# The same steps of an attention and feed-forward kernel, issued in a new order that holds 53 matmuls on zeros fewer

## The chip, the cores and the metric

The kernel runs on one core of one Trainium2 chip. Each core has five engines that work side by side: TensorE (PE, matmuls; its weight loads are shown apart as PEld), VectorE (DVE), ScalarE (ACT), GpSimd (POOL), and SyncE (SP), which here issues the transfers (DMAs). Each engine takes its instructions in the order in which the program issued them and waits where an operand isn't ready yet; engines meet only at such waits. The metric is device time in microseconds (us), median of several runs; less is better.

## The reference

Attention over a local window and a few global keys, with the result as the input of a feed-forward net:

```
q, k, v: (B=4, H=8, S=768, D=64) f32;  n_global = 8, n_local = 96
scores = q @ k^T / sqrt(D)
keep   = (key < n_global) | (0 <= query - key < n_local)
dist   = n_local where a key is global and not local, else |query - key|
scores = where(keep, scores - 2^-(h+1) * dist, -1e9)
a      = exp(scores - max(scores));  a = a / (sum(a) + 1e-9)
x      = (a @ v), heads side by side: (3072 tokens, 512)
h      = x @ w_in                                   # w_in (512, 2048)
g      = where(h >= 1, h, where(h <= -1, 0, (h + 1)^2 / 4))
out    = g @ w_out                                  # w_out (2048, 512)
```

`moe_w_in` and `moe_w_out` arrive as 64-bit floats, which the kernel takes apart as pairs of 32-bit words.

## The kernel before

**Halves.** A 32-bit product is made of three 16-bit ones: each operand is split into a high and a low f16 half, and high x high, high x low and low x high are summed in PSUM. The engines besides TensorE spend much of their work on splitting.

**Units and chunks.** The tokens lie in 24 units of 128 (one block of 128 queries of one batch, all eight heads); each unit has two halves of four heads. Two units make a chunk of 256 tokens for the feed-forward part, so there are 12 chunks.

**Steps.** Function `fast_path` doesn't issue instructions as it goes. It collects a list `plan` of steps, each a time, a function and its arguments, sorts the list by time (2808 steps), and then issues the steps in the order that the constant `PLACE` (L103) gives, a list of indices into the sorted plan:

```
1033    for n in PLACE or range(len(plan)):
1034        t, _, f, args = plan[n]
1037        f(*args)
```

So `PLACE` alone sets the order of each engine's queue. An index that it leaves out isn't issued. Which step runs on which engine:

- Weights: 32 pieces (0 to 15 of `w_in`, 16 to 31 of `w_out`). `w_load` (SP, L466) fetches a piece into one of three raw buffers; `w_bits` makes 32-bit floats of it in three DVE steps (L480, L484, L487) of 128x512; `w_hi` (ACT, L500) rounds to the high half, `w_scale` (ACT, L507) scales, `w_lo` (POOL, L514) subtracts to the low half. `check_load` (SP) and `check_reduce` (DVE, L546) read all weights once more to look at their range.
- Units 0 to 3 go a short way in f32: `first_scores` (8 matmuls, L567), `masked` (DVE, L578, bias, mask and maximum of one head), `expo` (ACT, L590), `norm` (two small DVE steps, L602 and L604), `first_turn` (four transposes on TensorE, L616), `first_pt` (ACT), `first_av` (8 matmuls, L634), `scale_x` (DVE, L642), `first_xt` (two transposes), `first_x` (ACT and DVE). `slope`, `positions`, `limits`, `distances` and `clip` build the bias.
- Units 4 to 23: `fetch` (SP), `conv_hi` (ACT), `conv_lo` (POOL L712 and L713, for v DVE L707), `keep_glob` and `set_glob` (DVE L740, L742) for the global keys; then `scores` (24 matmuls, L757), `masked`, `expo`, `norm`, `split_p` (ACT L773, then DVE L775), `turn_p` (SP, a transposing DMA, L782), `attend` (24 matmuls, L800), `scale_x`, `split_x` (ACT L814, DVE L816), `turn_x` (SP, a transposing DMA, L824).
- Feed-forward part: `ffn1(c,g)` (24 matmuls of 256 columns, L885, eight g in each chunk c) reads the transposed x of both units and two weight pieces; `gelu(c,g,s)` in five steps (ACT L898, DVE L903, DVE L908, ACT L912, POOL L916); `ffn2(c,t,f)` (three matmuls of 512 columns, L928; t is the unit of the chunk, f runs to 15) sums into PSUM; `finish` scales and stores.
- `filler` (L448) is one matmul of 512 columns on a tile of zeros into the tile `spare` (L443), whose result nobody reads; `warm` issues the same. The plan holds 150 `filler` steps, of which `PLACE` issues 101; eight `warm` calls of one matmul each come on top.

In this text `attend(5,0)` means that step for unit 5, half 0, and so on. The second `spare` tile serves as a buffer for every other `w_in` piece in `w_bits`, and in the rows on the tile `spare` these DVE steps stand under DVE.

**The first stage.** In the order before, TensorE has `positions`, `limits`, six `filler`, `first_scores(0,0)`, one `filler`, `first_scores(0,1)`, `first_turn(0,0)`, `first_turn(0,1)`, `first_av(0,0)`, `first_scores(1,0)`, one `filler`, `first_xt(0,0)`, seven `filler`, `first_av(0,1)`, and so on, with runs of up to 11 `filler` between the steps until about 75 us. `ffn1` begins at 32.04, `ffn2` of the first chunk at 75, and `ffn1` of the second at 80. The first `scores` of unit 4 stands at 100.3, the first `attend` at 126.45, and the last weight piece's `w_lo` at 120.7.

Of the kernel before, what the change touches and what calls it, by code (L numbers as in the profile page):

```python
# [103 lines left out]
    3, 0, 1, 2, 5, 7, 8, 71, 9, 4, 72, 11, 73, 74, 37, 6, 231, 300, 75, 10, 12, 13, 14, 19, 15, 16, 17, 18, 20,  # L104
    23, 76, 22, 21, 24, 27, 30, 25, 28, 32, 35, 34, 33, 29, 39, 45, 38, 41, 40, 48, 55, 49, 26, 36, 57, 31, 42,
    46, 54, 43, 47, 44, 52, 50, 53, 51, 334, 56, 223, 58, 77, 60, 78, 62, 63, 79, 59, 80, 81, 69, 64, 70, 82,
    61, 67, 359, 66, 65, 221, 83, 68, 227, 224, 241, 244, 225, 222, 240, 242, 84, 233, 226, 261, 234, 247, 236,
    238, 235, 228, 232, 289, 85, 237, 86, 248, 87, 243, 229, 290, 88, 246, 89, 230, 90, 249, 91, 250, 262, 239,
    253, 256, 92, 259, 394, 254, 260, 257, 245, 93, 94, 255, 263, 251, 266, 264, 268, 265, 252, 275, 269, 258,
    299, 270, 267, 95, 96, 302, 273, 272, 274, 305, 309, 97, 311, 278, 98, 347, 277, 360, 308, 286, 363, 279,  # L110
    313, 368, 365, 99, 315, 271, 422, 280, 100, 317, 372, 101, 276, 102, 366, 103, 373, 104, 282, 105, 375, 106,
    281, 291, 378, 326, 284, 285, 327, 385, 388, 288, 296, 318, 283, 413, 322, 287, 450, 107, 418, 331, 292,
    301, 108, 109, 421, 335, 110, 295, 111, 293, 294, 341, 298, 112, 304, 113, 114, 342, 297, 314, 115, 116,
    117, 310, 118, 119, 120, 303, 320, 325, 344, 307, 312, 329, 306, 319, 420, 316, 427, 330, 424, 321, 430,
    350, 336, 323, 328, 324, 426, 332, 333, 337, 431, 346, 338, 454, 339, 485, 340, 345, 121, 510, 343, 349,
    122, 123, 124, 348, 352, 357, 379, 440, 457, 351, 362, 125, 126, 356, 382, 127, 353, 355, 128, 129, 354,
    364, 391, 361, 130, 358, 131, 462, 132, 376, 133, 370, 134, 135, 136, 367, 380, 383, 369, 371, 374, 389,
    395, 381, 377, 392, 441, 459, 384, 467, 399, 386, 396, 390, 409, 387, 464, 393, 397, 398, 400, 407, 468,
    402, 401, 404, 406, 137, 138, 403, 410, 537, 433, 405, 411, 538, 419, 408, 139, 539, 140, 438, 141, 465,
    142, 412, 425, 416, 443, 414, 471, 143, 417, 144, 415, 145, 429, 146, 428, 147, 148, 423, 149, 150, 437,  # L120
    151, 432, 152, 153, 434, 439, 444, 445, 435, 436, 447, 446, 442, 448, 449, 478, 549, 451, 452, 470, 453,
    455, 590, 593, 456, 591, 598, 458, 154, 155, 461, 460, 466, 156, 157, 463, 473, 472, 480, 474, 553, 610,
    158, 603, 159, 160, 475, 161, 162, 163, 614, 469, 484, 481, 557, 164, 476, 487, 165, 166, 167, 479, 560,
    483, 168, 482, 169, 477, 170, 489, 171, 488, 486, 492, 607, 563, 515, 490, 633, 566, 494, 493, 517, 568,
    572, 491, 574, 498, 499, 495, 496, 500, 502, 497, 617, 503, 501, 577, 628, 504, 637, 507, 644, 505, 521,
    506, 508, 512, 511, 524, 669, 509, 518, 513, 527, 514, 651, 522, 523, 520, 519, 670, 526, 516, 654, 525,
    534, 528, 540, 530, 541, 542, 529, 664, 533, 543, 547, 531, 532, 658, 551, 536, 546, 555, 701, 535, 713,
    558, 704, 552, 698, 544, 718, 705, 545, 570, 564, 550, 556, 548, 575, 721, 579, 742, 567, 554, 583, 586,
    559, 571, 671, 752, 562, 565, 561, 576, 573, 569, 763, 585, 578, 600, 710, 580, 605, 589, 753, 770, 609,
    581, 595, 584, 582, 588, 615, 754, 587, 619, 785, 599, 592, 601, 596, 594, 597, 606, 604, 602, 630, 618,  # L130
    608, 811, 634, 611, 622, 639, 613, 612, 616, 623, 640, 621, 641, 620, 643, 652, 629, 647, 650, 624, 631,
    657, 649, 627, 635, 625, 636, 655, 638, 661, 653, 672, 663, 626, 660, 675, 747, 666, 632, 662, 681, 751,
    642, 680, 739, 682, 648, 645, 684, 741, 659, 690, 646, 694, 744, 683, 656, 691, 686, 674, 665, 673, 695,
    668, 667, 749, 712, 677, 678, 717, 676, 781, 679, 860, 692, 792, 685, 732, 697, 688, 687, 689, 702, 693,
    699, 696, 700, 715, 706, 703, 723, 707, 729, 708, 714, 711, 789, 727, 709, 735, 724, 716, 736, 743, 745,
    719, 734, 748, 726, 720, 722, 730, 756, 725, 738, 728, 760, 731, 750, 740, 733, 762, 757, 767, 755, 764,
    737, 766, 769, 758, 772, 768, 746, 773, 774, 759, 771, 761, 776, 775, 777, 780, 787, 779, 783, 784, 782,
    778, 791, 820, 765, 786, 788, 796, 790, 793, 799, 821, 804, 945, 823, 794, 946, 835, 827, 798, 795, 847,
    816, 805, 797, 814, 800, 810, 806, 801, 809, 817, 802, 803, 857, 808, 807, 813, 812, 851, 840, 815, 818,
    824, 819, 822, 859, 886, 861, 889, 825, 828, 833, 882, 826, 865, 831, 829, 978, 838, 845, 830, 832, 980,  # L140
    842, 837, 836, 841, 839, 844, 843, 862, 834, 846, 848, 984, 850, 849, 986, 852, 854, 912, 853, 855, 856,
    858, 863, 992, 864, 867, 866, 911, 915, 869, 871, 868, 936, 870, 874, 872, 878, 875, 876, 997, 879, 873,
    914, 880, 877, 995, 883, 891, 885, 881, 892, 938, 888, 884, 940, 893, 897, 887, 898, 890, 894, 904, 895,
    896, 917, 922, 899, 919, 1013, 920, 900, 1014, 907, 901, 923, 1021, 902, 906, 909, 903, 905, 910, 916, 996,
    908, 1023, 1015, 913, 918, 921, 961, 963, 924, 925, 928, 926, 933, 927, 929, 931, 930, 934, 942, 932, 1044,
    937, 947, 935, 1050, 948, 944, 1053, 951, 939, 941, 943, 1066, 950, 949, 956, 1063, 952, 1070, 953, 954,
    1075, 957, 958, 955, 1076, 964, 960, 959, 967, 966, 1026, 968, 1082, 962, 1089, 969, 965, 971, 998, 972,
    999, 970, 974, 1001, 973, 1002, 976, 1005, 1000, 975, 1004, 1003, 982, 977, 1108, 1007, 985, 979, 1109,
    1049, 1051, 1008, 981, 983, 1117, 1006, 1012, 989, 1009, 987, 991, 1119, 1010, 1020, 1011, 1016, 988, 1125,
    990, 993, 994, 1017, 1024, 1018, 1142, 1025, 1019, 1027, 1022, 1032, 1028, 1031, 1037, 1029, 1057, 1036,  # L150
    1033, 1038, 1040, 1043, 1060, 1041, 1046, 1148, 1100, 1101, 1030, 1047, 1152, 1034, 1045, 1058, 1035, 1077,
    1039, 1156, 1042, 1173, 1159, 1174, 1048, 1061, 1069, 1054, 1052, 1055, 1056, 1064, 1059, 1176, 1067, 1062,
    1072, 1065, 1073, 1068, 1074, 1071, 1083, 1078, 1081, 1088, 1079, 1087, 1090, 1205, 1084, 1095, 1092, 1206,
    1093, 1097, 1098, 1147, 1149, 1080, 1096, 1106, 1085, 1086, 1099, 1116, 1091, 1122, 1103, 1094, 1214, 1102,
    1104, 1110, 1124, 1112, 1105, 1150, 1114, 1216, 1107, 1111, 1120, 1113, 1237, 1121, 1115, 1123, 1118, 1130,
    1126, 1129, 1135, 1127, 1243, 1134, 1131, 1136, 1138, 1141, 1246, 1175, 1139, 1144, 1250, 1128, 1145, 1253,
    1195, 1196, 1132, 1143, 1157, 1133, 1265, 1137, 1140, 1266, 1146, 1160, 1166, 1268, 1153, 1151, 1154, 1155,
    1162, 1158, 1164, 1161, 1168, 1163, 1171, 1165, 1172, 1167, 1169, 1177, 1180, 1170, 1179, 1178, 1184, 1297,
    1183, 1185, 1181, 1188, 1186, 1187, 1298, 1191, 1192, 1242, 1244, 1182, 1189, 1203, 1190, 1306, 1194, 1193,
    1213, 1198, 1199, 1201, 1197, 1200, 1208, 1219, 1209, 1202, 1210, 1308, 1204, 1211, 1212, 1215, 1221, 1329,  # L160
    1224, 1223, 1229, 1231, 1226, 1227, 1236, 1233, 1234, 1267, 1228, 1239, 1335, 1207, 1289, 1247, 1240, 1290,
    1338, 1248, 1251, 1342, 1345, 1222, 1217, 1249, 1260, 1359, 1232, 1238, 1218, 1360, 1235, 1252, 1241, 1362,
    1255, 1220, 1257, 1245, 1225, 1254, 1256, 1230, 1258, 1259, 1262, 1261, 1263, 1269, 1264, 1391, 1270, 1272,
    1392, 1273, 1274, 1279, 1277, 1278, 1281, 1282, 1284, 1286, 1271, 1287, 1334, 1336, 1275, 1285, 1295, 1276,
# [1059 lines left out]
```

## Time and profile before

| what | value |
|---|---|
| runs | 628.42, 631.13, 628.40 us |
| median | 628.42 us |
| span of the profiled execution | 629.1 us |
| instructions | 14881 |
| TensorE busy | 615.7 us (98%) |
| DVE, ACT, POOL busy | 448.0, 418.7, 239.5 us |
| DMA | 88.08 MB, mean 140 GB/s |

The span is the time from the first to the last record of one profiled execution, 0.7 us above the median of the runs, which were timed without it. The profile gives each engine's busy time, the clock that TensorE was granted (1.00 is its full level of 2.4 GHz), and for each group of instructions what ended the idle time before it. Busy time is an average over stages with different limits, so views of single stretches are read beside it.

### The profile page before, as it was taken

The page shows a single profiled execution, that of the slowest core. Times are in us where ns is not written, and L with a number is a line of the kernel's source. Part 1 is how long each engine was busy: PE and PEld are TensorE (multiplying, and loading weights), DVE is VectorE, ACT ScalarE, POOL GpSimd, SP SyncE. Part 2 cuts the span into 40 slices and gives each one's busy share as a digit, 9 for nine tenths or more (in the row PEclk, how much of TensorE's full clock was granted, in tenths as well). Part 3 has the DMA queues.
Part 4 walks back from the last instruction along what each step waited for, and adds up shares of the span by engine and source line. Part 5 has one row for each costly group of instructions (what it writes and reads, how often), then busy time and mean ns, then how long its engine had stood idle before and what let it go on. Part 6 is the DMA issues. An engine that isn't in the chain of part 4 may idle for free. (4 is left out here: it accounts for less than half of the span.)

```text
span 629.1 us, 14881 instructions
## 1 busy us (share of the span) xinstructions
PE 615.7 (98%) x5665; PEld 420.8 (67%) x5665; DVE 448.0 (71%) x1150; ACT 418.7 (67%) x1070; POOL 239.5 (38%) x226
## 2 busy tenths in 40 slices
PE   7999999899999999999999999999999999999996
PEld 4676666556876767767757667667667767767652
DVE  6889999987676656665777777777777686663440
ACT  4778898997777776676686776766866765632220
POOL 0336786650544424433443333425324421122210
PEclk9999999999999999999999999999999999999999
DMA  6847566597533553464395497586476455361121
GB/s 201 261 144 225 187 227 221 129 170 157 126 87 77 91 121 93 80 148 111 69 231 154 94 208 186 127 186 175 110 177 183 112 140 137 76 150 69 51 69 38
DMA packets 144227, 88.08 MB, mean 140 GB/s; under 512 B 108180, under 2 KB 124820, under 8 KB 144148
## 3 DMA queue, kind: packets, MB, share of 16 engines
q1 hardware_dynamic: 144000, 86.92, 55.4%
q8 instruction: 46, 0.75, 0.5%
q14 instruction: 33, 0.27, 0.1%
q10 hardware_dynamic: 148, 0.13, 0.1%
HBM read 54.53 MB, written 6.29 MB: 97 GB/s over the span
## 5 line engine op out<-in xcount | busy, mean ns | idle before, releaser
L885 PE MATMUL h<-xt,wih 128*128 128x256 f16 x1536 | 256.4, 273 | 1.0 <-DVE u L908 0.9
L916 POOL TENSOR_TENSOR gl<-u,gh 128x512 f16<-128x512 f32 x96 | 117.4, 1224 | 284.9 <-ACT gh L912 274.6
L885 PE MATMUL h<-xt,wil 128*128 128x256 f16 x768 | 209.4, 273 | 0.0
L885 PEld LDWEIGHTS <-wih 128*128 128x128 f16 x1536 | 147.4, 98 | 30.9 <-DVE u L908 1.6
L928 PE MATMUL o<-wol,gh 128*128 128x512 f16 x384 | 145.6, 379 | 1.3 <-POOL wol L514 1.2
L928 PE MATMUL o<-woh,gh 128*128 128x512 f16 x384 | 145.8, 380 | 0.0
L928 PE MATMUL o<-woh,gl 128*128 128x512 f16 x384 | 145.6, 379 | 0.0
L928 PEld LDWEIGHTS <-gh 128*128 128x128 f16 x768 | 71.8, 98 | 67.3
L903 DVE SCALAR_TENSOR_TENSOR h<-h,u 128x512 f32<-128x512 f32 x96 | 66.7, 694 | 68.2 <-ACT u L898 68.0
L590 ACT ACTIVATE z<-z,nm 128x256 f32<-128x256 f32 (+1 forms) x192 | 91.7, 479 | 14.9 <-DVE nm L578 14.3
L912 ACT ACTIVATE gh<-u 128x512 f16<-128x512 f32 x96 | 60.2, 627 | 60.4 <-DVE u L908 60.1
L898 ACT ACTIVATE u<-h,half 128x512 f32<-128x512 f32 x96 | 64.9, 676 | 43.3 <-PE h L885 43.2
L578 DVE CUSTOM_DVE_ANT_0 z<-s,bias 128x256 f32<-128x256 f32 (+1 forms) x192 | 67.2, 396 | 26.6 <-PE s L757 23.2
L885 PEld LDWEIGHTS <-wil 128*128 128x128 f16 x768 | 75.0, 98 | 8.8
L775 DVE SCALAR_TENSOR_TENSOR ph<-z,ph 128x1024 f16<-128x1024 f32 x40 | 60.0, 1499 | 22.1 <-ACT ph L773 21.8
L928 PEld LDWEIGHTS <-gl 128*128 128x128 f16 x384 | 37.5, 98 | 47.2 <-issue 2.2
L908 DVE SCALAR_TENSOR_TENSOR u<-u,h 128x512 f32<-128x512 f32 x96 | 65.3, 681 | 3.3 <-DVE good L298 0.3
L546 DVE TENSOR_REDUCE sq<-c_raw 128x1 f32<-128x256 f32 x128 | 48.6, 408 | 0.2
L773 ACT ACTIVATE ph<-z 128x1024 f16<-128x1024 f32 x40 | 42.0, 1050 | 0.7
L757 PEld LDWEIGHTS <-qh 64*128 64x128 f16 x960 | 26.9, 94 | 16.7 <-issue 9.5
L800 PEld LDWEIGHTS <-pt 128*128 128x128 f16 x960 | 33.4, 98 | 7.0
L590 ACT ACTIVATION_READ_ACCUMULATOR z<-z,nm 128x1 f32 x192 | 36.0, 187 | 0.0
(101 smaller groups left out, 676.6 us busy)
## 6 DMA issues: line engine op xcount, KB each, us to landing
w_raw<-in_moe_w_in_dram SPq DMA_DIRECT2D x16, 512.0 KB, 3.8
w_raw<-in_moe_w_out_dram SPq DMA_DIRECT2D x16, 512.0 KB, 3.7
c_raw<-in_moe_w_in_dram SPq DMA_DIRECT2D x32, 256.0 KB, 3.5
c_raw<-in_moe_w_out_dram SPq DMA_DIRECT2D x32, 256.0 KB, 3.1
vr<-in_v_dram SPq DMA_DIRECT2D x28, 256.0 KB, 3.5
kr<-in_k_dram SPq DMA_DIRECT2D x28, 256.0 KB, 3.7
qr<-in_q_dram SPq DMA_DIRECT2D x24, 256.0 KB, 4.0
out_dram<-ob SPq DMA_DIRECT2D x23, 256.0 KB, 3.0
```

The source lines that it names most:

```text
L546: nc.vector.tensor_reduce(sq[:, col : col + 1], tops[n, e], axis=AX.X, op=op, apply_absolute_value=True)
L578: nc.vector.tensor_tensor_reduce(out=p32[u, hf][:, hh, :], in0=pts[u, hf][hh // 2][:, hh % 2, 0:n], in1=bias[:, 4 * hf + hh, base : base + n],
L590: nc.scalar.activation(z, z, AF.Exp, bias=nm[:, c : c + 1], scale=-1.0, accum_out=sums[:, c : c + 1])
L773: nc.scalar.activation(phs[u, hf][:, 0, :], zf, AF.Copy, scale=SP_)
L775: nc.vector.scalar_tensor_tensor(phs[u, hf][:, 1, :], zf, SP_, phs[u, hf][:, 0, :], op0=ALU.mult, op1=ALU.subtract)
L885: nc.tensor.matmul(hp[:, e, :], w[:, dc, f], xt[:, hf, 2 * a + j, :], start=(n == 0), stop=(n == 3 * NDC - 1),)
L898: nc.scalar.activation(us[c, g], hs[c, g], AF.Relu, bias=half, scale=2.0 / (SV * SW), accum_out=su[:, col : col + 1])
L903: nc.vector.scalar_tensor_tensor(ws[c, g], hs[c, g], 4.0 / (SV * SW), us[c, g], op0=ALU.mult, op1=ALU.max)
L908: nc.vector.scalar_tensor_tensor(dst, us[c, g], 4.0, ws[c, g], op0=ALU.min, op1=ALU.mult)
L912: nc.scalar.activation(gh, ws[c, g], AF.Copy)
L916: (nc.gpsimd if GL == "p" else nc.vector).tensor_sub(gl, ws[c, g], gt[c, g][0])
L928: nc.tensor.matmul(po, a[:, cs], w[:, f, :], start=(f == 0 and n == 0), stop=(f == NFC - 1 and n == 2))
```

## The change

Only `PLACE` is replaced. The old list has 2759 entries, the new one 2706. Both hold the same steps but for `filler`: 101 before and 48 after, so 109 and 56 matmuls on zeros with the eight of `warm`. The order is new nearly throughout; eight entries stand at the same position.

```
 PLACE = [
-    3, 0, 1, 2, 5, 7, 8, 71, 9, 4, 72, 11, 73, 74, 37, 6, 231, 300, 75, 10, 12, 13, 14, 19, 15, 16, 17, 18, 20,
-    23, 76, 22, 21, 24, 27, 30, 25, 28, 32, 35, 34, 33, 29, 39, 45, 38, 41, 40, 48, 55, 49, 26, 36, 57, 31, 42,
...
+    1, 3, 7, 2, 8, 0, 9, 37, 11, 241, 300, 5, 4, 6, 19, 18, 334, 14, 10, 12, 20, 13, 21, 17, 22, 16, 23, 24, 15, 25,
+    30, 27, 26, 289, 28, 31, 231, 71, 72, 73, 74, 29, 32, 42, 33, 44, 47, 66, 34, 75, 76, 77, 78, 359, 224, 53, 39,
+    35, 223, 41, 233, 36, 38, 236, 70, 79, 80, 81, 82, 83, 84, 85, 46, 43, 52, 40, 50, 246, 51, 56, 45, 59, 63, 48,
...
 ]
```

The indices say little by themselves. Decoded, TensorE's queue begins in the new order like this ("zeros x4" is four `filler` or `warm` matmuls):

```
positions, zeros x1, limits, first_scores(0,0), zeros x1, first_scores(0,1), zeros x4, first_turn(0,0),
zeros x12, first_av(0,0), first_scores(1,0), first_xt(0,0), zeros x4, first_turn(0,1), zeros x4, first_av(0,1),
first_scores(1,1), zeros x1, first_xt(0,1), zeros x2, first_turn(1,0), zeros x6, first_av(1,0), first_scores(2,0),
zeros x1, first_xt(1,0), zeros x4, first_turn(1,1), zeros x3, first_av(1,1), zeros x2, first_xt(1,1), zeros x5,
ffn1(0,0), ffn1(0,1), first_scores(2,1), first_turn(2,0), zeros x5, first_av(2,0), ffn1(0,2), first_xt(2,0),
ffn1(0,3), ffn1(0,4), first_scores(3,0), zeros x1, first_turn(2,1), first_av(2,1), ffn1(0,5), ... (no zeros after)
```

Beside the zeros, these things are moved:

- On DVE the three `w_bits` steps of the pieces come earlier among the steps of units 0 to 3: pieces 0 and 2 ahead of the first `scale_x`, 13 steps more ahead of `scale_x(2,0)`.
- Up to `attend(4,1)` both orders hold the same TensorE steps but for the zeros. On DVE, the new order has three `masked` and three `gelu` steps more ahead of `split_p(4,1,1)`, and one `conv_lo` and three `norm` less; ahead of `split_p(5,0,1)` it has two `gelu` steps and a `set_glob` more and one `norm` less. Ahead of `attend(5,0)`, TensorE has three `ffn2` steps less and two more.
- SP issues pieces 1 and 2 and a few later ones in another order, and weight loads change places with loads of k, q and v.
- In the later chunks `ffn2(c,0,...)` comes in longer runs before `ffn2(c,1,...)`, `turn_x` is issued ahead of a `turn_p`, and the matmuls that lie between the last `attend` of a chunk's units and the `ffn1` that reads them sum to 6.0 to 8.0 us in seven of the chunks 4 to 11 (8.7 to 10.6 in all but the last before).

## Rows read from the trace of the kernel before

**Rows 1.** The page of the profiled execution, parts 1 and 2: busy time and share of the span of each engine with its count of instructions, and the span in 40 equal slices, each digit a tenth of full clock granted (9 is 90% or more).

```profile
PE 615.7 (98%) x5665; PEld 420.8 (67%) x5665; DVE 448.0 (71%) x1150; ACT 418.7 (67%) x1070; POOL 239.5 (38%) x226
...
PEclk9999999999999999999999999999999999999999
```

**Rows 2.** Windows of the whole core. Columns: the stretch and its length, then busy time of PE, PEld, DVE, ACT and POOL (with the count of instructions), the granted clock of TensorE, the DMA share and GB/s.

```profile
45.00:75.00 30.00, 28.67 (x205) 19.73 (x203) 29.61 (x63) 23.74 (x55) 20.28 (x19) 1.00 0.63 202
...
60.00:80.00 20.00, 19.43 (x136) 13.25 (x136) 19.47 (x38) 16.23 (x40) 15.31 (x16) 1.00 0.65 217
...
75.00:118.00 43.00, 40.84 (x324) 27.86 (x322) 41.66 (x80) 40.32 (x97) 34.89 (x32) 1.00 0.68 213
...
160.00:620.00 460.00, 459.90 (x4388) 317.53 (x4385) 305.53 (x764) 289.15 (x734) 160.97 (x150) 1.00 0.52 124
```

**Rows 3.** A window of the tile `spare` alone. Columns: the stretch and its length, busy time of PE on it (the matmuls on zeros), of DVE on it (`w_bits` steps that use the second such tile), the granted clock, the DMA share and GB/s.

```profile
60.00:80.00 20.00, 6.91 (x29) 2.04 (x3) 1.00 0.65 217
```

**Rows 4.** The groups of instructions of equal form: the matmuls on zeros. Behind the count: busy time, mean ns of one, idle time before them.

```profile
L443 PE MATMUL spare<-zeros 128*128 128x512 f16 x109 | 30.5, 413 | 0.0
```

**Rows 5.** The timeline of TensorE, 0 to 40 us. Columns: start, duration to the end of the last one in the row, engine, line, operation, tiles, count.

```profile
10.76 1.32 PE L616 MATMUL tp<-ident,z 128*128 128x128 f32 x5
...
13.17 1.97 PE L634 MATMUL av<-vr,pt 128*128 128x64 f32 x8
...
17.05 3.09 PE L443 MATMUL spare<-zeros 128*128 128x512 f16 x7
19.98 1.00 PE L634 MATMUL av<-vr,pt 128*128 128x64 f32 x8
...
30.10 2.11 PE L443 MATMUL spare<-zeros 128*128 128x512 f16 x9
32.04 0.38 PE L885 MATMUL h<-xt,wih 128*128 128x256 f16 x2
```

**Rows 6.** The timeline of TensorE around 113 us. In brackets: the wait before, and what ended it.

```profile
112.43 0.38 PE L928 MATMUL o<-wol,gh 128*128 128x512 f16 x1 [0.93 <-POOL wol L514]
...
114.59 0.39 PE L885 MATMUL h<-xt,wih 128*128 128x256 f16 x2 [0.92 <-DVE u L908]
```

**Rows 7.** The timelines of DVE and TensorE before `attend(4,1)`: the copy of a global key, the last `split_p`, two steps of `gelu` with a `masked` between them, and the `attend`.

```profile
117.05 0.93 DVE L740 COPY kh<-kg 128x256 f16<-128x256 f16 x1
...
118.77 1.23 DVE L775 SCALAR_TENSOR_TENSOR ph<-z,ph 128x1024 f16<-128x1024 f32 x1
...
120.25 0.69 DVE L903 SCALAR_TENSOR_TENSOR h<-h,u 128x512 f32<-128x512 f32 x1
120.85 0.41 DVE L578 CUSTOM_DVE_ANT_0 z<-s,bias 128x256 f32<-128x256 f32 x1
121.19 0.68 DVE L908 SCALAR_TENSOR_TENSOR u<-u,h 128x512 f32<-128x512 f32 x1
...
126.45 0.86 PE L800 MATMUL av<-vh,pt 128*128 128x64 f16 x24
```

**Rows 8.** The timeline of DVE, 0 to 38 us: its larger waits, with what ended them, and the first `scale_x` (15.40).

```profile
8.62 0.29 DVE L578 CUSTOM_DVE_ANT_0 z<-s,bias 128x128 f32<-128x128 f32 x1 [0.65 <-PE s L567]
...
10.66 0.29 DVE L578 CUSTOM_DVE_ANT_0 z<-s,bias 128x128 f32<-128x128 f32 x1 [1.10 <-PE s L567]
...
12.67 0.17 DVE L602 TENSOR_SCALAR r<-sums 128x4 f32<-128x4 f32 x1 [0.92 <-ACT z L590]
...
15.40 0.41 DVE L642 TENSOR_TENSOR x<-av,r 128x256 f32<-128x256 f32 x1
...
21.02 0.42 DVE L642 TENSOR_TENSOR x<-av,r 128x256 f32<-128x256 f32 x1 [1.48 <-PE av L634]
...
29.93 0.29 DVE L578 CUSTOM_DVE_ANT_0 z<-s,bias 128x128 f32<-128x128 f32 x1 [0.65 <-PE s L567]
...
35.94 0.29 DVE L578 CUSTOM_DVE_ANT_0 z<-s,bias 128x128 f32<-128x128 f32 x1 [1.08 <-PE s L567]
...
37.32 0.42 DVE L642 TENSOR_TENSOR x<-av,r 128x256 f32<-128x256 f32 x1 [0.48 <-PE av L634]
```

**Rows 9.** The timelines of DVE, SP's queue and TensorE before `attend(5,0)`: `split_p`, the issue of `turn_p`, the `attend`.

```profile
125.19 1.22 DVE L775 SCALAR_TENSOR_TENSOR ph<-z,ph 128x1024 f16<-128x1024 f32 x1
126.49 1.46 SPq L782 DMA_TRANSPOSE pt<-ph  x1
...
132.56 0.63 PE L800 MATMUL av<-vh,pt 128*128 128x64 f16 x16
```

**Rows 10.** DMA issues by kind: tiles, the queue that issues, kind, count, KB each where known, median us from issue to landing.

```profile
w_raw<-in_moe_w_in_dram SPq DMA_DIRECT2D x16, 512.0 KB, 3.8
...
pt<-ph SPq DMA_TRANSPOSE x40, 4.5
...
xt<-xh SPq DMA_TRANSPOSE x40, 2.8
```

**Rows 11.** One later chunk, timelines of TensorE, DVE and SP's queue: the last `attend` of the chunk's units, the last `split_x`, the issue of `turn_x`, and the first `ffn1` that reads it.

```profile
273.04 0.86 PE L800 MATMUL av<-vh,pt 128*128 128x64 f16 x24
...
277.18 0.41 DVE L816 TENSOR_TENSOR xh<-x,xh 128x256 f16<-128x256 f32 x1
277.62 1.53 SPq L824 DMA_TRANSPOSE xt<-xh  x1
...
281.80 0.38 PE L885 MATMUL h<-xt,wih 128*128 128x256 f16 x2
```

281 rows, old and new, of the table PLACE are left out of this document.

## The prediction

> **What bounds the kernel now.** I read the busy shares first, then stretches of time. TensorE is busy 98% of the span and its granted clock is at the full level [rows 1]; from 160 to 620 us it is idle for 0.1 of 460 us [rows 2]. From there on the order of its work can neither gain nor lose much: the end comes when the work that is left has run. What can change is the time at which TensorE has its useful work of the first 130 us behind it. There it was busy too, but partly with matmuls on zeros: 109 in all, and between 60 and 80 us still 29 of them, 6.9 us of 20 [rows 3, 4]. At the full pace one takes 0.216 us: nine of them start at 30.10 and the next matmul at 32.04 [rows 5]. So about 23.5 us of its queue is filling.
>
> Filling is not what it waits for. From 45 to 75 VectorE (DVE) is busy 29.6 of 30 us, and from 75 to 118 41.7 of 43 [rows 2]: the conversion of the weights (three DVE steps for each of 32 pieces) has filled DVE since the start, and TensorE gets its operands as fast as DVE makes them. Where no zero matmul stood ready, TensorE waited in the open: 0.93 us for a converted piece and 0.92 us for a PSUM buffer that DVE had to free [rows 6]. So **DVE is the bound up to about 130 us, TensorE after that**, and the time is set by the place where one hands over to the other.
>
> **What the change removes.** 53 of the zero matmuls, 53 x 0.216 = 11.4 us of TensorE's queue. If TensorE were the bound there, the time would fall by 11.4 us. I count almost nothing of it: behind them stand matmuls whose operands come from DVE, and what was busy waiting becomes idle waiting. The eight `warm` calls stay.
>
> **What it moves, at the handing over.** I went through both lists entry by entry and compared what stands ahead of a step on its own engine.
>
> Gate 1 is `attend(4,1)`, TensorE at 126.45 [rows 7]. Ahead of it both lists hold the same TensorE work except the 53, so the same work is left. Its operand comes from `split_p(4,1,1)` on DVE (118.77 [rows 7]). The new list has three `masked` and three `gelu` steps more ahead of that and a `conv_lo` and three `norm` less. One `masked` takes 0.34 (120.85 to 121.19), one `gelu` step 0.60 (120.25 to 120.85) [rows 7]: 3 x 0.34 + 3 x 0.60 = 2.8 more; `conv_lo` has the shape of a `gelu` step, 0.6, and a `norm` step takes 0.17 (at 12.67 [rows 8]): 1.1 less. So 118.77 + 1.7 = 120.5.
>
> From `split_p` to `attend` I take the chain of unit 5: start 125.19, the transposing DMA issued 126.49, landing 4.5 after issue [rows 9, 10], so 5.8 us. Gate 1 opens at 126.3, against 126.45: -0.1.
>
> Gate 2 is `attend(5,0)`, TensorE at 132.56 [rows 9]. Two `gelu` steps and a `set_glob` (0.93, at 117.05 [rows 7]) are now ahead of `split_p(5,0,1)`, one `norm` less: 1.9 or 2.0, and I take 1.9. It moves to 127.1 and the gate to 132.9. Ahead of it TensorE has done one `ffn2` step less (0.65: three matmuls of 0.216): three were moved behind, two in front. So the end moves by 132.9 - 132.56 + 0.65 = **+0.9 us at gate 2**, the later one; everything else equal the new order loses.
>
> Not equal is how much DVE waits or is stretched on its way to the gates; call the difference X. Until 38 us its larger waits were 0.65, 1.10, 0.92, 1.48, 0.65, 1.08 and 0.48 [rows 8], together 6.4.
> - Up to `scale_x(0,1)` (21.02) the old waits sum to 4.15. The new list brings weight pieces 0 and 2 (six DVE steps) ahead of the places where the second and third arose, and has one zero matmul instead of six ahead of `first_scores(0,0)`: these three waits should go. But it puts 4 zero matmuls ahead of `first_turn(0,0)` and 12 between that and `first_av(0,0)`, where there were none. Before 20 us a zero matmul took 0.42 (seven from 17.05 to 19.98), twice the later 0.216 [rows 5], the two clock levels of 1.2 and 2.4 GHz for 512 columns. `first_scores(0,1)` ended at about 10.8; without the first wait and with four `slope` steps later on DVE I put it at 9.9. From there 4 x 0.42, four transposes 1.1 (five took 1.32 from 10.76) and 12 x 0.42 = 5.1, so 17.8, or 13.9 with everything at the full pace; then `first_av`, 1.97 (at 13.17) or 1.0 us (at 19.98) [rows 5]. DVE is at `scale_x(0,0)` at 15.40 - 2.67 (the three waits) + 1.5 (three conversion steps more, two `norm` less) = 14.2 [rows 8]. So it waits between 0.7 and 5.5 us; I take 4.1, the pace rising midway. Against 4.15 no gain; between -3.4 and +1.4.
> - The three waits from 29 to 38 us sum to 2.2. In the new list 13 conversion steps (7.8 us) more stand ahead of `scale_x(2,0)` and the scores of units 2 and 3 come later, so DVE has work while TensorE catches up: I take 0.2 left, -2.0, between -2.2 and 0.
> - From 75 to 118 DVE is idle 1.3 us [rows 2]. I take -0.8, between -1.3 and 0.
>
> Sum X = -2.8, bounds -6.9 and +1.4. The end moves by +0.9 - 2.8 = **-1.9 us**.
>
> **What else is moved, and its cover.** On SP's queue the weight loads keep their order but for pieces 1 and 2 and a few more, and change places with loads of k, q and v. A piece lands 3.8 us after its issue [rows 10], which waits for one of three raw buffers; by the sums DVE gets to each 0 to 1 us after it has landed. So nothing, up to +1 us, inside the bounds of X. In the later chunks `attend` of a chunk's last half unit stands closer to the `ffn1` that reads it: 6.0 to 8.0 us of matmuls in seven of the chunks 4 to 11 (`attend` 0.70 and nine `ffn2` of 0.65 in chunk 6), where it was 8.7 to 10.6 in all but the last. In the old trace this chain takes from 273.04 to 277.62, plus 2.8 for the DMA: 7.4, with `ffn1` at 281.80 [rows 10, 11]. That chain held a `split_p` and a `turn_p` ahead of the steps that count. In the new order it is `attend` 0.86, `scale_x` 0.42, other DVE steps of 0.3 to 1.0, 0.44 from `split_x` (277.18) to the issue and 2.8: 4.8 to 5.5 us [rows 8, 10, 11]. I take zero, with 0.5 us of cover and more in each. POOL, busy 20.3 of 30 and 34.9 of 43 us [rows 2], follows DVE step by step; its `w_lo` and `gelu` steps move with DVE's, and it has room: nothing. Steps of `check_load` and `check_reduce` lie on engines that are idle a third of that time [rows 2]: nothing.
>
> **The numbers.** The profiled execution has a span of 629.1 us, 0.7 above the median of the three runs, 628.42; some of what lies around the span is in neither. -1.9 from the median: **626.5 us**.
>
> **The rivals.**
> *A, faster: the zeros cost nothing at the start.* If TensorE's pace doubles as soon as the new run of zeros begins, `first_av(0,0)` starts near 13.9 and DVE waits 0.7 instead of 4.1: X = -6.2 and the time is 628.42 + 0.9 - 6.2 = 623.1. For it speaks that the run is longer than the seven after which the pace had risen [rows 5]; against it that the first 20 us never showed the full pace. It decides where the gain passes 3.1 us, at a wait under 3 us.
> *B, slower: the closer spacing in each chunk.* If the chain from `attend` to `ffn1` stays at the old 7.4 us, the spacings of 6.66, 6.53, 7.31, 6.66 and 6.01 cost 0.7 + 0.9 + 0.1 + 0.7 + 1.4 = 3.8 us, and TensorE, busy otherwise, never gets them back; with a quarter of X: 628.42 + 0.9 - 0.7 + 3.8 = 632.4. It decides wherever a chunk's spacing is less than the chain. For it: the old order kept 1.4 us of slack there [rows 10, 11]; against it: what was ahead in that chain now comes behind.
> *C, the clock.* Without filling, TensorE idles for 1 to 2 us at a time between 60 and 75 us. If the granted clock then fell to 1.2 GHz, its real work there, 19.4 - 6.9 = 12.5 us from 60 to 80 [rows 2, 3], would take up to twice as long. 6.9 us of that is room left by the zeros; the other 5.6 would be lost: 632.1. Against it: two open waits of 0.9 us passed with the full clock granted [rows 2, 6]. The Trainium skill (TensorE: Matmul & The Clock Gate, Part 1) says that half rate is the default, that activity lifts it and idle time brings it back; the rise from 0.42 to 0.216 us agrees, a fall is not in this trace.
> *D, nothing:* DVE's waits only change places (X near 0): 629.3.
>
> **How the numbers follow.** About 0.5% (3.1 us) is what a measurement of this kernel can tell from no change. Forecast (X from -1 to -4) 0.45, of which 0.04 lies below 625.3; A 0.26; B 0.14; C 0.05, of which 0.03 is beyond +3.1; D 0.10. So faster 0.30, same 0.53, slower 0.17. The range from A to B, 623.1 to 632.4, leaves out what exceeds them, about 0.15.
>
> **What would show it.** Right: far fewer than 109 zero matmuls and open TensorE waits between 55 and 80 us; DVE 97% busy to about 127; `attend(4,1)` near 124, `attend(5,0)` near 130; TensorE without idle after that. A shows as `first_av(0,0)` before 15 us. B shows as waits of `ffn1` on an `xt` transpose after 180 us. Wrong would be TensorE waits after 160 us on anything else, or DVE idle over 2 us between 40 and 118.

## The result, and the profile after

The changed kernel is **slower: 634.48 us (median of 5 runs, 632.33 to 636.21) against 630.32 (628.40 to 631.36); ratio 1.0067, interval 1.0040 to 1.0094.** Forecast were 626.5 us and a range of 623.1 to 632.4.

One thing has to be known to read the profiles. The times of the old kernel lie in two groups, 628.4 to 629.5 and 629.9 to 631.9 us, and its profiled execution is of the upper one: a run's time is 1.8 us above its span (628.80 and 627.0 in e5, 632.33 and 630.5 here), so the span of 629.1 belongs to 630.9. The changed kernel's profile, span 630.5, is the fastest of its five. So the profiles differ by 1.4 us only, the medians by 4.2. Three runs of the experiments (1055.69 us in e2, 643.85 and 908.78 us in e17) were slow ones, at a mean granted clock of 0.56, 0.95 and 0.66, and count in no ratio.

Windows of the changed kernel, columns as in [rows 2] (the line numbers in the rows differ by a few from kernel to kernel, since the list `PLACE` differs in length):

```profile
45.00:75.00 30.00, 24.40 (x189) 19.03 (x187) 28.09 (x70) 24.10 (x68) 17.75 (x18) 0.94 0.55 181
60.00:80.00 20.00, 15.36 (x115) 11.22 (x114) 19.75 (x44) 16.73 (x45) 14.35 (x15) 1.00 0.58 201
75.00:118.00 43.00, 40.11 (x357) 27.82 (x355) 42.01 (x80) 39.09 (x96) 32.29 (x29) 1.00 0.65 197
118.00:127.00 9.00, 6.11 (x66) 2.98 (x64) 8.71 (x25) 8.14 (x23) 4.65 (x4) 1.00 0.41 93
127.00:160.00 33.00, 31.49 (x328) 18.65 (x329) 20.11 (x66) 24.02 (x69) 8.26 (x8) 1.00 0.80 171
160.00:620.00 460.00, 460.00 (x4406) 319.03 (x4404) 303.40 (x771) 287.91 (x739) 163.19 (x150) 1.00 0.52 124
```

From 160 us on TensorE is as full as before: nothing was lost there. Up to 80 us it idles where the zeros stood. The loss is in the two rows between: 2.9 us of idle from 118 to 127 and 1.5 from 127 to 160, where there was 0.1 in both together before. Not all of these 4.4 us are lost, since TensorE had less work left there than before. Its timeline names the waits, DVE's the work behind them:

```profile
125.23 0.87 PE L796 MATMUL av<-vh,pt 128*128 128x64 f16 x24 [1.06 <-DMA pt<-ph]
...
127.54 0.84 PE L753 MATMUL s<-kh,qh 64*128 64x128 f16 x23 [1.28 <-DVE nm L574]
...
133.34 0.86 PE L796 MATMUL av<-vh,pt 128*128 128x64 f16 x24 [0.97 <-DVE x L638]
```

```profile
119.69 1.22 DVE L771 SCALAR_TENSOR_TENSOR ph<-z,ph 128x1024 f16<-128x1024 f32 x1
...
125.58 1.23 DVE L771 SCALAR_TENSOR_TENSOR ph<-z,ph 128x1024 f16<-128x1024 f32 x1 [0.29 <-ACT ph L769]
...
131.12 1.19 DVE L598 TENSOR_SCALAR r<-sums 128x4 f32<-128x4 f32 x2
...
132.77 0.42 DVE L638 TENSOR_TENSOR x<-av,r 128x256 f32<-128x256 f32 x1
```

The first is `attend(4,1)` (126.45 in [rows 7]; it is the second `attend`, the first, `attend(4,0)`, started at 119.38 before and at 114.29 here), the second `scores(6,0)`, the third `attend(5,0)` (132.56 in [rows 9]). On DVE: `split_p(4,1,1)`, 118.77 in [rows 7]; `split_p(5,0,1)`, 125.19 in [rows 9]; then a `norm` and `scale_x(4,1)`, which frees the buffer that `attend(5,0)` writes. Behind it TensorE has one `ffn2` step (0.65) more left than before, so the end moves by 133.34 - 132.56 + 0.65 = 1.43, and the span moved by 1.4. At `attend(4,1)`, with the same work done, the new order still led by 1.22 us. So all of the loss, 1.22 + 1.43 = 2.65 us, arises between these two steps.

### The profile page after: what moved, and what is told of

It reads as the page before. It is cut to its first block, busy times and chain, and to the rows that moved or that the text cites. A ratio compares the mean times of both kernels' runs of the same rounds, so it can differ in the third digit from the quotient of the medians.

```text
span 630.5 us, 14801 instructions
## 1 busy us (share of the span) xinstructions
PE 605.0 (96%) x5612; PEld 416.4 (66%) x5612; DVE 442.5 (70%) x1150; ACT 412.9 (65%) x1070; POOL 241.3 (38%) x226
## 4 chain that ended last, share of the span: by engine, by line
PE 81%; DVE 11%; ACT 3%; issue 2%; DMA 1%; ACTq 0%; DVEq 0%
PE o L924 36%; PE h L881 35%; PE s L753 4%; PE av L796 4%; DVE w_f L483 2%; DVE w_bits L476 2%; DVE w_bits L480 1%; DMA w_raw<-in_moe_w_out_dram 1%; DVE z L574 1%; PE av L630 1%; DVE h L899 1%; PE spare L439 1%; DVE u L904 1%; ACT wih L496 1%; ACT u L894 1%
## 5 line engine op out<-in xcount | busy, mean ns | idle before, releaser
L574 DVE CUSTOM_DVE_ANT_0 z<-s,bias 128x256 f32<-128x256 f32 (+1 forms) x192 | 70.8, 395 | 22.6 <-PE s L753 22.5
L771 DVE SCALAR_TENSOR_TENSOR ph<-z,ph 128x1024 f16<-128x1024 f32 x40 | 50.8, 1269 | 19.2 <-ACT ph L769 19.1
L542 DVE TENSOR_REDUCE sq<-c_raw 128x1 f32<-128x256 f32 x128 | 50.4, 410 | 3.8 <-DMA c_raw<-in_moe_w_out_dram 3.8
L796 PE MATMUL av<-vh,pt 128*128 128x64 f16 x960 | 34.5, 193 | 2.0 <-DMA pt<-ph 1.1
```

The lines of the kernel that those rows point to most:

```text
L574: nc.vector.tensor_tensor_reduce(out=p32[u, hf][:, hh, :], in0=pts[u, hf][hh // 2][:, hh % 2, 0:n], in1=bias[:, 4 * hf + hh, base : base + n],
L771: nc.vector.scalar_tensor_tensor(phs[u, hf][:, 1, :], zf, SP_, phs[u, hf][:, 0, :], op0=ALU.mult, op1=ALU.subtract)
L796: nc.tensor.matmul(av[:, hh, :], pt[:, a, hh, kt, :], vt[:, c, h * D : (h + 1) * D], start=(n == 0), stop=(n == 5),)
```

## The experiments

All edits change `PLACE` alone; they are shown by the names of the steps. Ratios are to the old kernel run beside them. "Old front" is the old order up to `ffn1(2,0)`.

**Which part of the list.**

e1:
```
 old order
-filler x53 (the last ones, from ahead of ffn1(0,1) to ahead of first_xt(3,1))
```


> The old order without its last 53 zero matmuls (from 47 us on), so that both kernels have 56. Theory O (the loss is made by the order at the handing over from DVE to TensorE, 1.4 us in the profiled pair; the zeros are free): ratio 1.000 within 0.003, though TensorE shows open waits of some 11 us between 47 and 75 us. Theory C (what the missing zeros cost is the clock: TensorE waits for over 1 us, its granted clock falls to 1.2 GHz for some us after it, differently in each execution): 2 to 4 us slower, ratio 1.003 to 1.006, and a granted clock under 1 in a stretch between 45 and 80 us.

Measured: 1.0019 (1.0003 to 1.0035). TensorE is busy 19.6 of 30 us from 45 to 75, its granted clock is 0.82 from 60 to 75, and `attend(4,1)` doesn't wait. Leaving the zeros out costs about 1.2 us (0.2 to 2.2 by the interval), the smaller part.

e5 and e4:
```
 PLACE = old order up to ffn1(2,0)   |  new order up to ffn1(2,0)
-        rest in the old order       | -rest in the new order
+        rest in the new order       | +rest in the old order
```


> The old order up to ffn1(2,0), with all its zeros, and behind it the new order. O and C: ratio 1.000 within 0.003, no TensorE idle after 160 us. B: slower by 1 to 4 us, ratio 1.002 to 1.006, with waits of ffn1 on a transposing DMA after 160 us.

> The new order up to ffn1(2,0) (about 155 us), and behind it all that is left in the old order. O and C: the whole loss is there, ratio 1.005 to 1.008. Theory B (the closer spacing of attend and ffn1 in the later chunks costs part of it): ratio 1.000 to 1.004.

Measured: e5 0.9987 (0.9970 to 1.0004), TensorE busy 460.0 of 460 us from 160 on; e4 1.0102 (1.0075 to 1.0129), even slower than the changed kernel, with a wait of 1.80 us before `ffn1(2,2)` where the two lists meet. So the front holds the whole loss and the spacing in the chunks none that e5 could tell: rival B is out.

e9, e10, e11 cut the front further:
```
e9   old order up to ffn1(1,0) (with 101 fillers), then the new one
e10  new order up to ffn1(0,0), old one up to ffn1(2,0), then the new one
e11  old order up to ffn1(0,0), then the new one
```


> The old order up to ffn1(1,0) (about 78 us, with all its 101 fillers), the new order behind it. Three places where the new order could lose: L, ahead of ffn1(0,0) (32.7 us in the changed kernel, 29.9 to 32.0 in the old order); M, from there to ffn1(1,0); N, behind ffn1(1,0), at the handing over from DVE to TensorE. L and M: ratio 0.997 to 1.001, TensorE without waits at 118 to 135 us. N: ratio 1.004 to 1.008, with waits before attend(4,1), scores(6,0) and attend(5,0) as in the changed kernel.

> The new order up to ffn1(0,0), behind it the old one up to ffn1(2,0) with its zeros, then the new one. L: ratio 1.003 to 1.007, the lead lost by ffn1(0,0) is still lost at attend(4,1). M and N: ratio 0.997 to 1.001.

> The old order up to ffn1(0,0), the new one behind it, with few zeros after 30 us. L: ratio 0.998 to 1.002. M or N: ratio 1.004 to 1.008. With e9 this parts M from N.

Measured: e9 1.0104 (1.0083 to 1.0126), e10 1.0056 (1.0034 to 1.0078), e11 1.0101 (1.0081 to 1.0121). The losses don't add up to that of the whole list, because each cut makes a misfit of its own (in e11 TensorE waits 5.20 us before `first_turn(2,0)`; in e10 DVE's waits up to `split_p(4,1,1)` sum to 11.0 us, 6.3 in the changed kernel), so e10 and e11 are no clean verdict. e9 is the clearest: its list and its times are those of the old kernel's profile up to `ffn1(1,0)` (80.16 and 80.22 us), and behind that its span grew by 5.4 us, which speaks for N, the handing over. That also holds a misfit, a DVE wait of 2.4 us for `gelu(1,0,1)` where it was 0.44. TensorE's timeline in e9:

```profile
128.13 0.86 PE L798 MATMUL av<-vh,pt 128*128 128x64 f16 x24 [2.41 <-DVE x L640]
...
130.57 1.46 PE L755 MATMUL s<-kh,qh 64*128 64x128 f16 x23 [1.42 <-DVE nm L576]
...
132.37 0.63 PE L926 MATMUL o<-wol,gh 128*128 128x512 f16 x1
132.79 0.63 PE L926 MATMUL o<-woh,gl 128*128 128x512 f16 x1
...
136.24 0.38 PE L926 MATMUL o<-woh,gl 128*128 128x512 f16 x1
136.46 0.38 PE L926 MATMUL o<-woh,gh 128*128 128x512 f16 x1
```

After the two waits the `ffn2` matmuls start every 0.43 us instead of every 0.22, from 131.97 to 135.78; with the `scores` before them that is 5.2 us at half pace. The window says so too (columns as in [rows 2]; a granted clock of 0.74 over 13 us is about 7 us at the lower level, waits included):

```profile
127.00:140.00 13.00, 10.46 (x118) 6.04 (x119) 10.40 (x36) 11.24 (x32) 6.25 (x6) 0.74 0.70 154
```

5.2 us at half pace are 2.6 us lost, and here TensorE is the bound from then on.

**Are zeros the remedy?** e2:
```
 new order
+filler x5 ahead of first_turn(2,1), x8 ahead of first_av(2,1),
+filler x4 ahead of first_turn(3,0), x10 ahead of first_av(3,0)
```


> The new order with 27 zero matmuls more, put ahead of four steps before which TensorE waited: 5 before first_turn(2,1), 8 before first_av(2,1), 4 before first_turn(3,0), 10 before first_av(3,0). O: as the changed kernel, ratio 1.005 to 1.008. C: the granted clock is 1.00 from 45 to 80 us, the ffn1 behind first_av(2,1) runs at full pace, and about half of the loss is gone: ratio 1.001 to 1.004.

Measured: 1.0071 (1.0044 to 1.0097). The changed kernel's clock falls early as well, after a wait of 1.47 us:

```profile
53.06 1.56 PE L630 MATMUL av<-vr,pt 128*128 128x64 f32 x8 [1.47 <-ACT pt L619]
54.41 0.64 PE L881 MATMUL h<-xt,wih 128*128 128x256 f16 x2
...
56.97 0.38 PE L881 MATMUL h<-xt,wih 128*128 128x256 f16 x2
...
65.17 1.10 PE L630 MATMUL av<-vr,pt 128*128 128x64 f32 x8 [1.97 <-ACT pt L619]
```

(The longer wait before the last of these rows was followed by no fall: the granted clock is 1.00 from 60 to 75.) In e2 the fall is gone (granted clock 1.00 from 45 to 75), and the steps behind it come no earlier: `scores(4,0)` starts at 94.21 us, 94.14 in the changed kernel. So the fall costs nothing there: DVE is the bound. The time of e2 alone wouldn't show this, since its clock fell elsewhere, behind a wait of 2.42 us before `attend(4,1)` (TensorE's timeline, and a window of TensorE: busy time, clock, DMA share, GB/s):

```profile
125.59 1.44 PE L797 MATMUL av<-vh,pt 128*128 128x64 f16 x24 [2.42 <-DVE x L639]
```

```profile
126.00:130.00 4.00, 3.21 (x46) 0.50 0.66 186
```

That put `attend(5,0)` at 134.61, 1.27 later than in the changed kernel.

**Missing cover at the gates.** e3:
```
 new order, DVE
+norm(4,1) x2, scale_x(4,1)
 masked(6,0,0), masked(6,0,1), masked(6,0,2), conv_lo(6,v), ... 
-norm(4,1) x2, scale_x(4,1)
```


> The new order with norm(4,1) (both steps) and scale_x(4,1) moved ahead of masked(6,0,0) on DVE, past a conv_lo and four masked steps. In the trace of the changed kernel attend(5,0) waits 0.97 us for the PSUM buffer that scale_x(4,1) frees. Theory G (that buffer is the gate): the wait is gone, 1 us less than the changed kernel, ratio to the old kernel 1.004 to 1.006. Rival H (behind it the transposed operand of attend(5,0) is as late, or the moved steps only shift the wait): ratio 1.006 to 1.008, the same.

Measured: 1.0084 (1.0058 to 1.0109), no gain that the timing tells. The wait itself is gone:

```profile
126.18 0.87 PE L796 MATMUL av<-vh,pt 128*128 128x64 f16 x24 [1.06 <-DMA pt<-ph]
...
133.15 0.86 PE L796 MATMUL av<-vh,pt 128*128 128x64 f16 x24
```

From `attend(4,1)` to `attend(5,0)` it is 6.97 us instead of 8.11. The profiled execution reached `attend(4,1)` 0.95 later, so the end is the same. G is shown for the wait, not for the time.

e13 and e14:
```
 e13: e3, and on TensorE
+ffn2(1,0,0)
 attend(4,1)
+ffn2(1,0,1), ffn2(1,0,2), ffn2(1,0,3)
 scores(6,0)
-ffn2(1,0,0) ... ffn2(1,0,3)
 e14: e13
-filler x15 (first_scores(0,1) to first_av(0,0))
```


> The new order with ready work in front of the three last waits: on TensorE ffn2(1,0,0) moved ahead of attend(4,1), and ffn2(1,0,1) to ffn2(1,0,3) ahead of scores(6,0); on DVE norm(4,1) and scale_x(4,1) ahead of masked(6,0,0). K (what is missing there is ready work): the waits of 1.06, 1.28 and 0.97 us shrink to under 1 in sum, the granted clock stays at 1.00 from 120 to 140 us, 2 to 4 us less than the changed kernel, ratio 1.000 to 1.004. Q (DVE is late and the waits come back at the next step): ratio 1.005 to 1.009.

> The same, and without the 15 zero matmuls between first_scores(0,1) and first_av(0,0). K: as e13 or up to 1.5 us less, ratio 0.998 to 1.003. Q: 1.004 to 1.007.

Measured: e13 1.0037 (1.0024 to 1.0049), all nine runs between 631.4 and 632.7; e14 1.0027 (1.0010 to 1.0044). In e13:

```profile
126.48 0.38 PE L924 MATMUL o<-woh,gh 128*128 128x512 f16 x1 [0.48 <-ACT ob L941]
127.13 0.86 PE L796 MATMUL av<-vh,pt 128*128 128x64 f16 x24
...
133.37 0.87 PE L796 MATMUL av<-vh,pt 128*128 128x64 f16 x24 [1.26 <-DMA pt<-ph]
```

Though its DVE came to `split_p(5,0,1)` 1.8 us later than in the changed kernel's profile (127.41), `attend(5,0)` stands at the same place and now waits for its operand, not the buffer. From these steps on the waits are 1.74 instead of 3.31, and the clock is 1.00 from 118 to 142 us. e13 differs from e3 by the four `ffn2` steps alone, and their intervals don't touch. So ready work in front of the waits does gain (K): nearly half of the loss by the ratios, though the interval of e13 still overlaps that of the changed kernel (1.0040 to 1.0094). The gain is in the slower executions: the profiled spans are alike, 630.6 and 630.5 us, but the runs of the changed kernel go up to 636.2. The rest fits DVE's lateness (Q): `scores(5,1)`, ahead of these steps, waited 1.34 here, 0.50 in the changed kernel.

**DVE's own lateness.** e6 and e7:
```
 e6: new order                      | e7: old front, new rest
+distances(False), clip(False), slope(False,0..7)
 scale_x(0,0)                       |  norm(0,1)
...
-distances(False), clip(False), slope(False,0..7)   (at 62 to 87 us)
```


> The new order with distances(False), clip(False) (DVE) and the eight slope(False) steps (ACT) moved ahead of the first scale_x, where DVE waited 1.7 us and POOL has little to do. In the changed kernel these two DVE steps took 2.79 and 3.45 us at 68 to 81 us, because single instructions of 0.3 us lasted up to 1.27 us and ended with an instruction of POOL. Theory S (DVE comes 3 us late to the handing over, in part since POOL stretches it): the steps take 2.9 us together, the wait of 1.7 is filled, split_p(4,1,1) stands 3 to 5 us earlier, TensorE's waits of 3.3 us at 125 to 133 us shrink to under 1, ratio 0.999 to 1.003. Rival (the order at the gates themselves is the loss, whatever DVE's lead): the same waits there, ratio 1.005 to 1.008.

> The old order up to ffn1(2,0) and the new one behind it (0.9987 of the old kernel), with distances(False), clip(False) and the slope(False) steps moved ahead of norm(0,1), where DVE waited 0.9 us. S: these steps take 2.9 instead of 4.4 us, DVE is 2 us earlier at 110 us, TensorE's waits there (1.9 us) go, ratio 0.995 to 0.998. Rival (TensorE is the bound there): 0.998 to 1.000.

Measured: e6 1.0094 (1.0065 to 1.0123), e7 1.0066 (1.0048 to 1.0084). In the changed kernel, DVE and then POOL (L402 and L418 are instructions of these two steps, POOL's are those that run beside them):

```profile
69.29 1.27 DVE L402 TENSOR_SCALAR m<-m 128x256 f32<-128x256 f32 x1
...
79.54 1.26 DVE L418 SCALAR_TENSOR_TENSOR m<-m,nval 128x256 f32<-128x256 f32 x1
```

```profile
69.25 1.16 POOL L510 TENSOR_TENSOR wol<-w_f,woh 128x512 f16<-128x512 f32 x1
...
79.31 1.20 POOL L709 TENSOR_TENSOR kh<-kr,kh 128x512 f16<-128x512 f32 x1
```

and in e6, with POOL idle:

```profile
15.03 0.29 DVE L402 TENSOR_SCALAR m<-m 128x256 f32<-128x256 f32 x1
...
17.38 0.48 DVE L418 SCALAR_TENSOR_TENSOR m<-m,nval 128x256 f32<-128x256 f32 x1
```

The steps fell from 6.2 to 2.8 us, as expected: beside POOL the two DVE instructions ended 0.15 and 0.29 us after POOL's. So engines don't meet only at waits for operands; one also stretches the other's instructions. The Trainium skill (GPSIMD Engine Reference, Specifications) says that the two engines share their SBUF interfaces and that DVE instructions with two SBUF inputs or in a two-port mode contend there. The rows of L418, which has two such inputs, agree; L402 has one, and no run here shows its mode. But DVE's waits grew from 6.3 to 11.1 us: eight more ACT steps and 2.8 us of DVE work stood in the chain of unit 0, and `ffn1(0,0)` came at 39.3 instead of 32.7. In e7 `first_av(0,0)` waited 4.84 us for ACT. S's expectation of the time failed by where I put the steps.

e12 puts them elsewhere, e15 takes zeros out on top:
```
 e12: old front, new rest
+distances(False)      ahead of masked(2,1,0)
+clip(False)           ahead of masked(3,0,0)
 e15: e12
-filler x17 (ahead of first_turn(3,0), first_av(3,0), ffn1(0,5))
```


> The old order up to ffn1(2,0) and the new one behind it (0.9987 of the old kernel), with distances(False) moved ahead of masked(2,1,0) and clip(False) ahead of masked(3,0,0), two places where DVE waited 0.65 and 1.07 us for scores; the slope steps stay. S (DVE's lateness at the handing over is what costs): the two steps take 2.9 instead of 4.4 us and fill two waits, DVE is 2 to 3 us earlier at 110 us, TensorE's last waits (0.94 and 0.93 us at 110 and 113) go: ratio 0.995 to 0.998. Rival (the waits come back behind, as they did when the steps stood at 13 us): 0.999 to 1.004.

> The kernel e12 (old order up to ffn1(2,0), distances(False) and clip(False) moved to where DVE waited), without the 17 zeros ahead of first_turn(3,0), first_av(3,0) and ffn1(0,5). If zeros on TensorE ate DVE's lead there (DVE waited 2.2 us for first_xt(3,0)), that wait shrinks and the kernel is 2 to 3 us faster than e12: ratio 0.996 to 1.000. If the lead is eaten by TensorE's useful work or the clock: as e12, 1.002 to 1.005.

Measured: e12 1.0034 (1.0017 to 1.0051), e15 1.0023 (1.0009 to 1.0036): the rival's side. The two steps took 4.3 us as in e5 (4.4), so they weren't shortened at all, `ffn1(0,0)` now waits 1.05 us, and DVE's waits grew to 10.9 us (2.21 of it before `first_x(3,0)`), 8.1 in e15, where e5 has 6.8. No placing of these steps paid.

**The start.** e8:
```
 new order
-filler x15 (first_scores(0,1) to first_av(0,0))
```


> The new order without the 15 filler matmuls on zeros that stand between first_scores(0,1) and first_av(0,0). Theory Z (they only hold up TensorE, and with it DVE's first scale_x, 1.7 us of wait): first_av(0,0) near 13.5, the wait gone, ratio 1.003 to 1.006. Rival W (they are what brings TensorE's clock to the full level early): the granted clock stays at half for longer, matmuls of the units 0 and 1 take twice as long, ratio 1.007 to 1.012.

Measured: 1.0051 (1.0033 to 1.0070), in Z's range, but not clear of the changed kernel's interval; `first_av(0,0)` at 13.30. W is half right: that step took 1.97 us, 1.00 behind the zeros. Either way `split_p(4,1,1)` stood at 119.7.

e16 and e17 (on e5):
```
 positions
+filler x2
 limits
 filler x6 (e17: x4)
 first_scores(0,0)
 filler
+filler x1 (e17: the two from above)
 first_scores(0,1)
```


> The kernel e5 (old order up to ffn1(2,0), new behind it) with two fillers more ahead of limits, where TensorE waited 1.2 us, and one more ahead of first_scores(0,1), where it waited 0.27 us. Theory P (the activity before 9.4 us decides when the pace rises, and that makes the two groups): the pace rises by 9.4 us in most executions, times in one group at 628.2 to 629.0, ratio to the old kernel 0.996 to 0.998. Rival (the groups have another cause): two groups as before, ratio 0.998 to 1.000.

> The kernel e5 with two fillers more ahead of limits, and two of those ahead of first_scores(0,0) moved behind it, ahead of first_scores(0,1). P, and DVE's first wait of 0.65 us is filled: as e16 or up to 0.6 us less, ratio 0.995 to 0.998. Rival: 0.998 to 1.001.

Measured: **e16 0.9978 (0.9965 to 0.9990), 628.68 us, all twelve runs between 628.3 and 629.3**: the upper group is gone (five of e5's twelve runs took 629.7 us or more), and no other version has a lower ratio, though the intervals of e5 and e17 overlap its own. e17 0.9980 (0.9963 to 0.9997), median 628.6 of ten, still in two groups (four of ten at 630.4 to 630.5). TensorE in e5, to be set beside [rows 5]:

```profile
9.40 0.92 PE L565 MATMUL s<-kr,qr 64*128 64x128 f32 x8 [0.27 <-DVE nm L576]
...
15.66 1.67 PE L441 MATMUL spare<-zeros 128*128 128x512 f16 x7
17.54 1.10 PE L632 MATMUL av<-vr,pt 128*128 128x64 f32 x8 [0.21 <-DVE xt L664]
```

With the same list up to here, seven zeros took 1.67 us where they took 3.09, and `first_av(0,1)` stands 2.4 us earlier. In e16 it is between the two:

```profile
16.50 2.14 PE L441 MATMUL spare<-zeros 128*128 128x512 f16 x7
18.47 1.00 PE L632 MATMUL av<-vr,pt 128*128 128x64 f32 x8
```

The granted clock of the windows doesn't tell the old kernel and e5 apart: from 10 to 20 us it is 1.00 in both, so the pace is read from the matmuls themselves. In e16 it is 0.83 there. More profiles of lists that begin like the old one fit groups made by an early or a late rise: the seven zeros took 1.67 us in e1 and e15, whose profiled runs lie low among their own (629.90 and 630.26 us), and 3.19 in e12, where it lies high (632.89). In e9 and e11 they took 3.02 and 3.19, and the six runs of each show no two groups. In e17 they took 2.29, about as in e16, and its run lies in the upper group (630.40). So the cause of the groups is argued, from one profile of each list. That the pace rises by 9.4 us in e16 is not what its profile shows; that its runs stay in the lower group is measured.

## Why the prediction was wrong

- **The bound held.** DVE up to about 130 us, TensorE after it, and the end as gate time plus work left: 0.78 + 0.65 at gate 2 is the whole 1.4 us between the profiles.
- **The first step that failed is X**, forecast at -2.8. From the order alone `split_p(4,1,1)` should move by +1.7, with X to 117.7; it stood at 119.69. Its DVE work came out as reckoned, +1.8 (steps present in one order only). DVE's waits of 0.1 us and more up to there fell from 8.8 to 6.3, in sum nearly as forecast. But steps common to both lists took 1.9 us longer, 1.28 of it in `clip(False)` and 0.54 in `distances(False)`: what POOL runs beside DVE changed. I took DVE's durations as fixed. X was about -0.8 (119.69 - 118.77 - 1.7).
- **The sum of the waits was partly luck.** Up to `scale_x(0,1)` they fell by 2.1 us, where none was forecast (2.0 are left of 4.15), and between 45 and 60 us there are 1.8 us of new ones, where the forecast had none. With these, DVE's idle time from 45 to 118 us is 2.9 us (28.09 of 30 and 42.01 of 43), 1.7 before [rows 2]: more than the 2 us that the prediction itself named as a sign of being wrong.
- **And X's waits were read from one execution.** The 1.48 us before `scale_x(0,1)` is absent in e5, with the same list: it goes with the late rise of TensorE's pace in the profiled execution. Against e5 the waits fell only from 6.8 to 6.3, and its `attend(5,0)` stands at 130.49, 2.85 earlier than the changed kernel's; with 0.65 that is the 3.5 us between the spans, 627.0 and 630.5. My base was one of the slower executions. TensorE in e5:

```profile
124.37 0.86 PE L798 MATMUL av<-vh,pt 128*128 128x64 f16 x24
...
130.49 0.86 PE L798 MATMUL av<-vh,pt 128*128 128x64 f16 x24
```

- **The second step that failed is gate 2, which had a second lock.** I followed only the operand: 125.58 + 5.8 = 131.4. `attend(5,0)` also needs the buffer that `scale_x(4,1)` frees, which the new list puts behind `conv_lo`, and started at 133.34, 1.9 later. By e3, where the buffer is free early, the buffer makes 1.1 of this (8.11 - 6.97); the other 0.8 is TensorE's own queue, which the wait before `scores(6,0)` had put back. Of the 3.2 us by which gate 2 missed the forecast (130.1), these make 1.9 and `split_p(5,0,1)`, forecast at 124.3, makes 1.3. There X's miss, 2.0, is made smaller by a wrong price: the `set_glob` taken at 0.93 took 0.13 until the next step began.
- **`scores(6,0)`** wasn't looked at: in the old order three `ffn2` steps stand between it and `attend(4,1)`, in the new none, and it waits 1.28. That e13 gained with work in front of these waits shows the missing cover.
- **The clock** was rival C, in the wrong place. At 53 us a fall costs nothing (e2). Behind the gate it cost 2.6 us in e9. That the slower executions of the changed kernel lose their further 2 to 4 us in this way fits e2 and e9, and their mean granted clock, 0.986 to 0.994 where the fastest has 0.995. But the one at 0.994 is 2.1 us longer too, and no trace shows where their clock fell: argued, not shown.
- Rival A, the run of zeros at the start: `first_av(0,0)` started at 15.28, between its two cases, and DVE waited 1.7 instead of 4.1. Rival B: no (e5). The zeros at 1.2 us in e1: small, and not nothing.
- Open: how the 4.2 us divide between DVE's lateness and missing cover. e13 gave back 0.3% of 0.67%; no experiment took the lateness away alone, since the attempts (e6, e7, e12) made waits elsewhere.

## What to carry over

Where one engine hands the bound to another, list for each gate all that opens it (operand, output buffer, PSUM for the step after) and the ready work that stands in front: a microsecond of lead elsewhere is worth nothing if three steps in a row wait there. Waits of the profile that a change is to save should first be seen in a second execution of the same list. And a new order changes durations too, where two engines' instructions run beside each other in new pairs.

## What the runs showed of the hardware

- TensorE's granted clock fell to half behind waits: 1.47 us of wait and about 3 us at half in the changed kernel (0.89 from 45 to 60 us), 2.41 and 1.42 us of wait and about 7 at half in e9 (0.74 from 127 to 140), 2.42 us and about 7 in e2 (0.83 from 120 to 140). The Trainium skill (TensorE: Matmul & The Clock Gate, Part 1) says that the clock returns to half when the engine idles; the fall that [rows 1] don't show is here.
- The length of a wait alone doesn't tell whether the clock falls. In the changed kernel 1.97 us at 65.17 passed at 1.00. In e17 the clock fell at 113 us (0.89 from 105 to 120) behind waits of 0.94 and 0.92 us, and the old kernel passed two such waits at 1.00 [rows 2, 6].
- The early pace isn't fixed: a list that is the same up to `ffn1(2,0)` had full pace from 9.4 us in one execution (e5) and from about 20 in another [rows 5], and `attend(5,0)` stood 2.07 us apart (132.56 and 130.49). With three zero matmuls more in TensorE's idle time before 9.4 us, all twelve runs lay in the faster group (e16).
- DVE instructions of 0.29 and 0.48 us took 1.27 and 1.26 us beside POOL's, 4.4 and 2.6 times as long.
